# Feed-forward weights decoded without GpSimd, and the norms of blocks 1 and 2 on VectorE

## Chip, cores and metric

One core of a Trainium2 chip. The metric is the device time of one execution of the whole program in microseconds (us), as the median of several runs. TensorE multiplies matrices, VectorE and ScalarE work elementwise, GpSimd too; SyncE only issues DMAs here. A kernel instance has one queue per engine, and each engine takes its instructions in the order of its queue.

## What is computed

Three stages follow each other on 8 batches of 576 tokens and 512 features. First a linear attention: softmax of q over the features and of k over the tokens, in 8 heads of 64. Then a feed-forward stage, which is the one that matters here:

```python
X = np.fft.fft(np.fft.fft(x, axis=1), axis=2)
u = x + np.real(X)
un = (u - mean(u)) / np.sqrt(var(u) + 1e-06)
x = u + np.maximum(un @ w_ch1, 0.0) @ w_ch2     # 512 -> 2048 -> 512
```

Last a gated stage: two token-shift mixes, `k = max(xk @ w_k, 0)`, and the output `sigmoid(xr @ w_r) * (k*k @ w_v)`. The weights arrive as float64 and are read by the kernel as pairs of 32-bit words.

## The kernel before, in words

The 4608 tokens are cut into nine blocks of 512. `front_x` does the attention of batch after batch, `front_y` the two Fourier transforms as matrix products (`transform`) and then the norm of each block whose batches are done (`norm`), `front_z` the feed-forward weights. These are generators. They are stepped by hand before the blocks, until the norm of block 0 and the first six weight pieces are issued (lines 971 to 978), and later by `side()` between the matrix products of the blocks (`mm1`, `mm2`), so that attention and transforms of later batches lie beside the feed-forward products of earlier blocks. This gives the order in which work is traced. A scheduler of the framework then orders the queue of each engine: work traced earlier has priority, work traced later fills in. Batch 1's attention is traced after block 0's norm and the weights, and can be placed among them.

Feed-forward weights: each of the 32 pieces (16 of `w_ch1`, 16 of `w_ch2`, 128 x 512) is loaded as 512 pairs of words into one of four places. `decoded` (line 178) makes a float32 bit pattern of each pair: ScalarE turns the low word into a number of 0 to 7 (L194), VectorE shifts and masks the high word (L195), then merges the sign and top bit (L196), and GpSimd adds the low part (L197). `squares` (L202) then sums each piece's squares on ScalarE; after all 16 pieces of a matrix `scales` makes its power-of-two scale (L211 to L221). `split` (line 223) writes each piece as two float16 parts, high and rest, into a place whose last reader is the split before it:

```python
if c % 4 == 1:
    nc.scalar.activation(out=h, in_=st, func=AF.Copy, scale=s)
    nc.vector.scalar_tensor_tensor(out=l, in0=st, scalar=s, in1=h, op0=ALU.mult, op1=ALU.subtract)
else:
    nc.scalar.activation(out=st, in_=st, func=AF.Copy, scale=s)
    nc.scalar.activation(out=h, in_=st, func=AF.Copy)
    nc.gpsimd.tensor_tensor(out=l, in0=st, in1=h, op=ALU.subtract)
```

These are L229, L230 (8 pieces) and L232, L233, L234 (24 pieces). The first products of a block (L1034) need the normed tokens in two float16 parts (`halves_part`, L642 on ScalarE and L643 on VectorE) and a split `w_ch1`; the second products (L1057) need a split `w_ch2`.

Norms: `norm_part` sums a token's features (L577, L579), takes the mean off (L589), squares on ScalarE (L591, L592), sums again (L595, L596), makes the reciprocal root (L611 to L626) and multiplies (L629). In block 0 TensorE does the sums and VectorE the product. For blocks 1 and 2 sums and product are on GpSimd; from block 3 on the sums are on GpSimd, the product on VectorE. Blocks 0 and 1 go in two parts of 256 tokens, the rest whole.

GpSimd has other work too: a subtraction or product for three halves of the attention (L329, L343), the maximum over partitions for batches 3 to 7 (L323, traced in the front strand), and one step in the decoding of the last stage's weights (`decode`, L167).

Of the kernel before, what the change touches and what calls it, by code (L numbers as in the profile page):

```python
# [13 lines left out]
AF = mybir.ActivationFunctionType  # L14
ALU = mybir.AluOpType
# [15 lines left out]

MAX_PE = (0, 1, 2)

POOL_N = (1, 2)
SUMS_PE = (0,)
SUMS_F32 = (0, 1)

# [7 lines left out]
def net(ctx, tc, q, k, v, w1, w2, mu_k, mu_r, w_k, w_v, w_r, ce_d, se_d, cs_d, ss_d, alt_d, id_d, out):  # L45
    nc = tc.nc
# [18 lines left out]
    def aside(first, strand):  # L65


        turn_of[0] += 1
        if not first:
            return bank(f"side{turn_of[0] % 2 if done_block[0] < 0 else strand}", 1)  # L70
        x = turn_of[0] % 6
        return bank(f"side{x // 3}", 1) if x in (0, 3) else bank(f"acc{(1, 2, 4, 5).index(x)}", 1)
# [3 lines left out]
    def segments(i):  # L76

        t0, n = blocks[i]
        done, found = 0, []
        while done < n:  # L80
            b, s = divmod(t0 + done, S)
            m = min(n - done, S - s)
            found.append((b, s, m, done))
            done += m
        return found
# [86 lines left out]
    def spare_words():  # L172

        if not spare:
            spare.append(up.tile([128, 4, S], F32, tag="u", name="words").rearrange("p t s -> p (t s)").bitcast(U32))
        return spare[0]

    def decoded(w, c):


        z = places[0] % 4
        places[0] += 1
        if z < 2:
            raw = wst.tile([128, 512, 2], U32, tag="raw", name="raw", bufs=2)
        else:
            raw = spare_words()[:, 1024 * (z - 2):1024 * (z - 1)].rearrange("p (n w) -> p n w", w=2)
        if w == 0:
            src = w1.bitcast(U32)[128 * (c % 4):128 * (c % 4) + 128, 1024 * (c // 4):1024 * (c // 4) + 1024]
        else:
            src = w2.bitcast(U32)[128 * c:128 * c + 128, :]  # L190
        nc.sync.dma_start(out=raw.rearrange("p n w -> p (n w)"), in_=src)
        x = wr[:, place[w, c] + 1]
        hi, lo = raw[:, :, 1], raw[:, :, 0]
        nc.scalar.activation(out=lo, in_=lo, func=AF.Copy, scale=2.0 ** -29)  # L194
        nc.vector.tensor_scalar(out=x, in0=hi, scalar1=3, scalar2=0x3FFFFFFF, op0=ALU.logical_shift_left, op1=ALU.bitwise_and)  # L195
        nc.vector.scalar_tensor_tensor(out=x, in0=hi, scalar=0xC0000000, in1=x, op0=ALU.bitwise_and, op1=ALU.bitwise_or)  # L196
        nc.gpsimd.tensor_tensor(out=x, in0=x, in1=lo, op=ALU.add)  # L197

    def squares(w, c):

# [22 lines left out]
    def split(w, c):  # L223
        k = place[w, c]
        st = wr[:, k + 1].bitcast(F32)
        s = wsc[:, 3 * w + 1:3 * w + 2]
        h, l = wf[:, k, 0:512], wf[:, k, 512:1024]
        if c % 4 == 1:
            nc.scalar.activation(out=h, in_=st, func=AF.Copy, scale=s)  # L229
            nc.vector.scalar_tensor_tensor(out=l, in0=st, scalar=s, in1=h, op0=ALU.mult, op1=ALU.subtract)  # L230
        else:
            nc.scalar.activation(out=st, in_=st, func=AF.Copy, scale=s)  # L232
            nc.scalar.activation(out=h, in_=st, func=AF.Copy)  # L233
            nc.gpsimd.tensor_tensor(out=l, in0=st, in1=h, op=ALU.subtract)  # L234

    def w1t(t, f):

# [39 lines left out]
    def mark(name, *ins):  # L277
        marks[name] = ins
# [277 lines left out]
    def mean(i, sq, cs, n):  # L556

        pt = aside(i == 0, 1)
        if i < 2:
            mm(out=pt[:, 0:n], lhsT=ones, rhs=sq[:, 0, cs], start=True, stop=True)  # L560
        else:
            hl = hp.tile([128, 2, 512], F32R, tag="rs", name="hl", bufs=1)
            h, l = hl[:, 0, cs], hl[:, 1, cs]
            nc.scalar.activation(out=h, in_=sq[:, 0, cs], func=AF.Copy)
            nc.vector.tensor_tensor(out=l, in0=sq[:, 0, cs], in1=h.bitcast(F32), op=ALU.subtract)
            mm(out=pt[:, 0:n], lhsT=onesr, rhs=h, start=True, stop=False)
            mm(out=pt[:, 0:n], lhsT=onesr, rhs=l, start=False, stop=True)
        return pt

    def norm_part(i, sq, d, rs, c0, n):  # L570
        segs = [(b, s + max(c0 - o, 0), min(o + m, c0 + n) - max(o, c0), max(o, c0)) for b, s, m, o in segments(i) if o < c0 + n and o + m > c0]
        cs = slice(c0, c0 + n)
        tt = nc.vector.tensor_tensor
        add = nc.gpsimd.tensor_tensor if i else tt
        onpe = i in SUMS_PE
        for b, s, m, o in segs if not onpe else ():
            add(out=sq[:, 0:2, o:o + m], in0=U[b][:, 0:2, s:s + m], in1=U[b][:, 2:4, s:s + m], op=ALU.add)  # L577
        if not onpe:
            add(out=sq[:, 0, cs], in0=sq[:, 0, cs], in1=sq[:, 1, cs], op=ALU.add)  # L579
            yield 0  # L580
            yield 0
            pt = mean(i, sq, cs, n)
        else:
            pt = aside(i == 0, 1)
            for b, s, m, o in segs:
                for t in range(4):
                    mm(out=pt[:, o - c0:o - c0 + m], lhsT=ones, rhs=U[b][:, t, s:s + m], start=(t == 0), stop=(t == 3))
        for b, s, m, o in segs:
            mv = tt(out=d[:, :, o:o + m], in0=U[b][:, :, s:s + m], in1=pt[:, None, o - c0:o - c0 + m].to_broadcast([128, 4, m]), op=ALU.subtract)  # L589
        yield 1  # L590
        nc.scalar.activation(out=sq[:, 0:2, cs], in_=d[:, 0:2, cs], func=AF.Square)  # L591
        ma = nc.scalar.activation(out=sq[:, 2:4, cs], in_=d[:, 2:4, cs], func=AF.Square)  # L592
        yield 0
        if not onpe:
            add(out=sq[:, 0:2, cs], in0=sq[:, 0:2, cs], in1=sq[:, 2:4, cs], op=ALU.add)  # L595
            add(out=sq[:, 0, cs], in0=sq[:, 0, cs], in1=sq[:, 1, cs], op=ALU.add)  # L596
            yield 0
            yield 0
            pt = mean(i, sq, cs, n)
        else:  # L600
            pt = aside(i == 0, 1)
            for t in range(4):
                mp = mm(out=pt[:, 0:n], lhsT=ones, rhs=sq[:, t, cs], start=(t == 0), stop=(t == 3))
            if i == 0:
                mark(5, mv, ma, mp)
        if rs is None:
            rs = hp.tile([128, 2, 512], F32, tag="rs", name="rs", bufs=1)
        v, r = rs[:, 0, cs], rs[:, 1, cs]
        w = sq[:, 1, cs]
        if i in SUMS_F32:  # L610
            nc.scalar.activation(out=r, in_=pt[:, 0:n], func=AF.Ln, bias=wsc[:, 7:8])  # L611
            nc.scalar.activation(out=r, in_=r, func=AF.Exp, scale=-0.5)
            yield 1
            tt(out=v, in0=r, in1=r, op=ALU.mult)
            nc.vector.scalar_tensor_tensor(out=v, in0=pt[:, 0:n], scalar=1e-6, in1=v, op0=ALU.add, op1=ALU.mult)
            nc.vector.tensor_scalar(out=v, in0=v, scalar1=-0.5, scalar2=1.5, op0=ALU.mult, op1=ALU.add)
            tt(out=r, in0=r, in1=v, op=ALU.mult)
        else:
            nc.vector.tensor_scalar(out=v, in0=pt[:, 0:n], scalar1=1e-6, scalar2=None, op0=ALU.add)
            nc.scalar.activation(out=r, in_=v, func=AF.Ln)  # L620
            nc.scalar.activation(out=r, in_=r, func=AF.Exp, scale=-0.5)
            yield 1

            tt(out=w, in0=r, in1=r, op=ALU.mult)
            nc.vector.scalar_tensor_tensor(out=w, in0=w, scalar=-0.5, in1=v, op0=ALU.mult, op1=ALU.mult)
            nc.vector.scalar_tensor_tensor(out=r, in0=w, scalar=1.5, in1=r, op0=ALU.add, op1=ALU.mult)  # L626
        yield 0
        for x in range(2):
            (nc.gpsimd.tensor_tensor if i in POOL_N else tt)(out=d[:, 2 * x:2 * x + 2, cs], in0=d[:, 2 * x:2 * x + 2, cs], in1=r[:, None, :].to_broadcast([128, 2, n]), op=ALU.mult)  # L629
            yield 0  # L630
        if i == 0:
            halves_part(0, c0, n)
# [291 lines left out]
    def front_z():  # L924
        for w in range(2):
            for c in range(17):
                if c < 16:
                    decoded(w, c)
                if c > 0:
                    squares(w, c - 1)  # L930
                yield 0
            scales(w)
            yield 0
        for c in range(4):
            split(0, c)
            yield 0
        for c in range(2):
            split(1, c)
            yield 0
# [387 lines left out]
```

## Time and profile before

| | us |
|---|---|
| median of 3 runs | 1511.14 (1507.36 to 1512.99) |
| the profiled execution, its own time | 1508.74 |
| its span, first to last instruction | 1507.0 |
| TensorE busy in the span | 1413.3 |
| VectorE busy | 1018.2 |
| ScalarE busy | 677.1 |
| GpSimd busy | 224.2 |

The profiled execution took 1.7 us outside its span. An engine counts as busy while an instruction of it runs, and an instruction that is held up after its start counts as running. The granted clock of TensorE is a share of full speed (2.4 GHz), mean 0.971 over the span.

### The profile page before, as it was taken

How to read it: one execution, taken by the hardware profiler on the slowest of the kernel's cores; microseconds unless marked ns; L12 is line 12 of the kernel's file. 1: busy time of each engine (PE TensorE's matmuls, PEld its weight loads, DVE VectorE, ACT ScalarE, POOL GpSimd, SP SyncE). 2: the span in 40 equal slices, each digit the busy share in tenths (PEclk: the TensorE clock that was granted, in tenths of full speed). 3: DMA queues.
4: the chain of work that ended last, by engine and by line, in shares of the span. 5: the costliest groups of instructions: out<-in, count | busy, mean ns of one | idle time of the engine just before them, and what ended most of it. 6: DMA issues, size and time to landing. Idle time of an engine off the chain costs nothing. (4 is left out here: it accounts for less than half of the span.)

```text
span 1507.0 us, 21074 instructions
## 1 busy us (share of the span) xinstructions
PE 1413.3 (94%) x8453; PEld 879.8 (58%) x8453; DVE 1018.2 (68%) x1770; ACT 677.1 (45%) x1237; POOL 224.2 (15%) x180
## 2 busy tenths in 40 slices
PE   3464999999999999999999999999999999999998
PEld 2343888879655655555555444444666666666665
DVE  6997747758477485674452457775899789776643
ACT  5568544434233333332321236554666556564432
POOL 1553532022020010100100204311000000000000
PEclk8586999999999999999999999999999999999999
DMA  8462003211102111101001103410211011100001
GB/s 307 153 219 92 1 1 107 70 50 51 62 16 78 36 48 44 50 34 44 1 11 46 37 29 119 137 46 4 80 35 49 31 57 57 36 22 29 29 15 42
DMA packets 38237, 89.47 MB, mean 59 GB/s; under 512 B 5083, under 2 KB 11516, under 8 KB 38140
## 3 DMA queue, kind: packets, MB, share of 16 engines
q1 hardware_dynamic: 38140, 88.14, 17.2%
q8 instruction: 66, 1.08, 0.3%
q14 instruction: 31, 0.25, 0.1%
HBM read 69.25 MB, written 18.87 MB: 58 GB/s over the span
## 5 line engine op out<-in xcount | busy, mean ns | idle before, releaser
L1034 PE MATMUL h<-unh,wr 128*128 128x512 f16 (+1 forms) x1408 | 381.6, 342 | 1.1 <-ACT unh L642 1.1
L1057 PE MATMUL acc<-hh,wr 128*128 128x512 f16 (+1 forms) x1408 | 370.9, 342 | 3.2 <-DVE wkl L748 2.7
L1034 PEld LDWEIGHTS <-wr 128*128 128x128 f16 x2112 | 203.5, 98 | 171.8 <-issue 11.7
L1057 PEld LDWEIGHTS <-wr 128*128 128x128 f16 x2112 | 203.4, 98 | 164.3 <-DVE wkl L748 3.0
L1034 PE MATMUL h<-unl,wr 128*128 128x512 f16 (+1 forms) x704 | 240.6, 342 | 5.2 <-DVE unl L643 5.2
L1057 PE MATMUL acc<-hl,wr 128*128 128x512 f16 (+1 forms) x704 | 221.5, 342 | 0.0
L1160 PE MATMUL acc<-ring,last 128*128 128x512 f16 x864 | 201.2, 379 | 0.2 <-DVE last L1191 0.2
L1040 DVE SCALAR_TENSOR_TENSOR hl<-h,hh 128x512 f16<-128x512 f32 x144 | 99.1, 688 | 144.5 <-ACT hh L1039 143.5
L1039 ACT ACTIVATE hh<-h 128x512 f16<-128x512 f32 x144 | 85.2, 592 | 162.7 <-PE h L1034 162.4
L1160 PEld LDWEIGHTS <-last 128*128 128x128 f16 x864 | 84.0, 98 | 86.5 <-DVE last L1191 0.7
L1095 PEld LDWEIGHTS <-wkh 128*128 128x128 f16 x1008 | 98.5, 98 | 34.1
L1148 PE MATMUL side<-ring,x 128*128 128x512 f16 x432 | 101.1, 379 | 0.0
L1189 ACT ACTIVATE last<-last,pw 128x512 f32<-128x512 f32 x72 | 51.6, 717 | 106.9 <-DVE last L1188 106.3
L1095 PE MATMUL h<-x,wkh 128*128 128x256 f16 x560 | 95.7, 273 | 0.0
L1110 DVE TENSOR_TENSOR last<-h,last 128x512 f32<-128x512 f32 x90 | 61.8, 687 | 49.9 <-PE h L1095 49.8
L1095 PE MATMUL h<-x,wkl 128*128 128x256 f16 x280 | 76.3, 273 | 0.0
L1095 PE MATMUL h<-last,wkh 128*128 128x256 f16 x448 | 76.1, 273 | 0.0
L1148 PEld LDWEIGHTS <-x 128*128 128x128 f16 x432 | 42.3, 98 | 42.5
L1191 DVE TENSOR_TENSOR last<-last 128x512 f16<-128x512 f32 x72 | 49.4, 687 | 22.1 <-ACT last L1190 21.7
L1095 PE MATMUL h<-last,wkl 128*128 128x256 f16 x224 | 61.1, 273 | 0.0
L577 POOL TENSOR_TENSOR sq<-u 128x384 f32<-128x384 f32 (+7 forms) x16 | 24.9, 1558 | 209.5 <-DVE u L522 100.8
L854 ACT ACTIVATE aa<-y,ms 128x512 f32<-128x512 f32 x72 | 48.0, 712 | 17.5 <-DVE x L862 12.2
(349 smaller groups left out, 2298.9 us busy)
## 6 DMA issues: line engine op xcount, KB each, us to landing
vt<-in_v_dram SPq DMA_DIRECT2D x16, 650.0 KB, 5.0
kt<-in_k_dram SPq DMA_DIRECT2D x16, 576.0 KB, 3.9
qt<-in_q_dram SPq DMA_DIRECT2D x16, 576.0 KB, 3.9
out_dram<-oo SPq DMA_DIRECT2D x36, 256.0 KB, 2.0
y<-yT SPq DMA_DIRECT2D x8, 1026.0 KB, 5.3
raw<-in_w_dram SPq DMA_DIRECT2D x16, 512.0 KB, 3.8
words<-in_w_dram SPq DMA_DIRECT2D x16, 512.0 KB, 4.5
raw<-in_w_k_dram SPq DMA_DIRECT2D x16, 256.0 KB, 3.5
```

The lines of the kernel that those rows point to most:

```text
L577: add(out=sq[:, 0:2, o:o + m], in0=U[b][:, 0:2, s:s + m], in1=U[b][:, 2:4, s:s + m], op=ALU.add)
L854: nc.scalar.activation(out=a, in_=y[:, t, 0:n], func=AF.Copy, scale=mu[:, w, 1, t:t + 1])
L1034: mm(out=pt[:, o:o + m], lhsT=a, rhs=c[:, t, o:o + m], start=(t == z == 0), stop=(t == 3 and z == 2))
L1039: ma = nc.scalar.activation(out=hh[:, 0:n], in_=pt[:, 0:n], func=AF.Relu)
L1040: mv = nc.vector.scalar_tensor_tensor(out=hl[:, 0:n], in0=pt[:, 0:n], scalar=0.0, in1=hh[:, 0:n], op0=ALU.max, op1=ALU.subtract)
L1057: mm(out=acc[x][:, o:o + m], lhsT=a, rhs=c[:, o:o + m], start=(f == z == o == 0), stop=(f == NF - 1 and z == 2), skip_group_check=(i < 2))
L1095: mm(out=pt[:, 256 * x:256 * x + 256], lhsT=c[:, u, 128 * x:128 * x + 128], rhs=d[:, u], start=(fresh and x == u == z == 0), stop=(last an ...
L1110: nc.vector.tensor_tensor(out=out, in0=view(pt), in1=addend, op=ALU.add)
L1148: mm(out=pt, lhsT=a[:, v, u, c, o:o + 128], rhs=w[:, t, :], start=(t == y == 0), stop=(t == 3 and y == 2))
L1160: mm(out=acc[x], lhsT=a[:, 128 * x:128 * x + 128], rhs=c[:, f, :], start=(f == z == 0), stop=(f == 7 and z == 2))
L1189: nc.scalar.activation(out=o, in_=o, func=AF.Square, scale=W["pw"][:, 10 + g:11 + g])
L1191: nc.vector.tensor_tensor(out=l2, in0=o, in1=h2, op=ALU.subtract)
```

## The change

The set of blocks whose product is on GpSimd becomes empty, and the sums go to GpSimd only from block 3 on. In `decoded` ScalarE's scale and bias are chosen so that the low part comes out complemented to 7, and VectorE puts it into the three free low bits with an exclusive-or and an or in one instruction; the instruction on GpSimd goes. In `split` all 32 pieces take the form that eight had. `decode`, for the last stage's weights, stays as it is.

```diff
-POOL_N = (1, 2)
+POOL_N = ()
...
-        nc.scalar.activation(out=lo, in_=lo, func=AF.Copy, scale=2.0 ** -29)
+        nc.scalar.activation(out=lo, in_=lo, func=AF.Copy, scale=-0.9975 * 2.0 ** -29, bias=7.49)
...
-        nc.gpsimd.tensor_tensor(out=x, in0=x, in1=lo, op=ALU.add)
+        nc.vector.scalar_tensor_tensor(out=x, in0=lo, scalar=7, in1=x, op0=ALU.bitwise_xor, op1=ALU.bitwise_or)
...
-        if c % 4 == 1:
-            nc.scalar.activation(out=h, in_=st, func=AF.Copy, scale=s)
-            nc.vector.scalar_tensor_tensor(out=l, in0=st, scalar=s, in1=h, op0=ALU.mult, op1=ALU.subtract)
-        else:
-            nc.scalar.activation(out=st, in_=st, func=AF.Copy, scale=s)
-            nc.scalar.activation(out=h, in_=st, func=AF.Copy)
-            nc.gpsimd.tensor_tensor(out=l, in0=st, in1=h, op=ALU.subtract)
+        nc.scalar.activation(out=h, in_=st, func=AF.Copy, scale=s)
+        nc.vector.scalar_tensor_tensor(out=l, in0=st, scalar=s, in1=h, op0=ALU.mult, op1=ALU.subtract)
...
-        add = nc.gpsimd.tensor_tensor if i else tt
+        add = nc.gpsimd.tensor_tensor if i > 2 else tt
```

## Rows read from the trace of the kernel before

**Rows 1.** The page, part 1: busy us (share of the span) xinstructions.
```profile
PE 1413.3 (94%) x8453; PEld 879.8 (58%) x8453; DVE 1018.2 (68%) x1770; ACT 677.1 (45%) x1237; POOL 224.2 (15%) x180
```

**Rows 2.** Busy time by stretch: length, PE, PEld, DVE, ACT, POOL, PEclk, DMA share, GB/s.
```profile
28.00:136.00 108.00, 50.57 (x203) 38.08 (x201) 103.55 (x156) 73.17 (x160) 56.68 (x36) 0.65 0.50 166
136.00:210.00 74.00, 69.22 (x563) 60.43 (x563) 40.12 (x73) 43.89 (x82) 33.34 (x25) 0.96 0.08 26
210.00:260.00 50.00, 50.00 (x436) 44.52 (x434) 33.60 (x59) 20.11 (x33) 13.96 (x13) 1.00 0.20 65
```

**Rows 3.** Timeline, 118 to 140 us: start, us, engine, line; [idle before <-releaser].
```profile
133.74 0.37 PE L1034 MATMUL h<-unl,wr 128*128 128x256 f16 x1 [5.23 <-DVE unl L643]
```

**Rows 4.** The same view, GpSimd and VectorE, 118 to 140 us.
```profile
128.90 1.34 POOL L197 TENSOR_TENSOR wr<-wr,words 128x512 uint32<-128x512 uint32 x1 [1.28 <-ACT unh L642]
129.02 1.77 DVE L196 SCALAR_TENSOR_TENSOR wr<-words,wr 128x512 uint32<-128x512 uint32 x1
```

**Rows 5.** VectorE's groups by form, 28 to 136 us: xcount | busy us, mean ns.
```profile
L196 DVE SCALAR_TENSOR_TENSOR wr<-raw,wr 128x512 uint32<-128x512 uint32 x16 | 14.3, 893 | 0.1
L196 DVE SCALAR_TENSOR_TENSOR wr<-words,wr 128x512 uint32<-128x512 uint32 x16 | 13.7, 874 | 0.0
L195 DVE TENSOR_SCALAR wr<-words 128x512 uint32<-128x512 uint32 x16 | 11.0, 692 | 2.0 <-DMA words<-in_w_dram 1.9
L195 DVE TENSOR_SCALAR wr<-raw 128x512 uint32<-128x512 uint32 x16 | 10.6, 662 | 0.8 <-DMA raw<-in_w_dram 0.8
L435 DVE TENSOR_TENSOR eo<-u 128x288 f32<-128x288 f32 x8 | 5.2, 695 | 0.0
L629 DVE TENSOR_TENSOR d<-d,rs 128x512 f32<-128x512 f32 x4 | 4.7, 1226 | 0.0
...
L307 DVE TENSOR_REDUCE m<-kt 128x256 f32<-128x1024 f32 x2 | 3.9, 1970 | 0.1
...
L451 DVE TENSOR_TENSOR el<-eo,eh 128x289 fp32r<-128x289 f32 x4 | 2.9, 723 | 0.0
...
L319 DVE TENSOR_TENSOR m<-ident,wsc 128x256 f32<-128x256 f32 x2 | 1.9, 966 | 0.0
L617 DVE TENSOR_TENSOR rs<-rs 128x256 f32<-128x256 f32 x2 | 1.9, 962 | 0.0
L614 DVE TENSOR_TENSOR rs<-rs 128x256 f32<-128x256 f32 x2 | 1.9, 956 | 0.0
...
L359 DVE COPY kvbd<-kvbd 64x2 f32<-64x2 f32 x1 | 1.2, 1236 | 0.0
...
L513 DVE TENSOR_TENSOR sd<-pc,acc 128x290 f32<-128x290 f32 x2 | 0.9, 452 | 0.0
...
L490 DVE TENSOR_TENSOR yl<-acc,yh 128x256 fp32r<-128x256 f32 x2 | 0.8, 419 | 0.0
```

**Rows 6.** Lines L195, L196 and L230 alone: duration ns min/median/max.
```profile
L195 DVE TENSOR_SCALAR wr<-raw x16: 399/415/1516, 27.9 to 121.0; 128x512 uint32<-128x512 uint32 x16
L196 DVE SCALAR_TENSOR_TENSOR wr<-raw,wr x16: 675/680/1708, 28.3 to 125.2; 128x512 uint32<-128x512 uint32 x16
L230 DVE SCALAR_TENSOR_TENSOR wr<-wr,wsc x8: 739/752/2285, 134.2 to 200.6; 128x512 f16<-128x512 f32 x8
```

**Rows 7.** Timeline, VectorE, a pair of merges back to back.
```profile
42.40 1.29 DVE L196 SCALAR_TENSOR_TENSOR wr<-words,wr 128x512 uint32<-128x512 uint32 x2
```

**Rows 8.** Timeline, 312 to 348 us, VectorE, GpSimd and TensorE.
```profile
332.60 1.23 DVE L333 TENSOR_TENSOR kt<-kt,m 128x1024 f32<-128x1024 f32 x1 [3.39 <-POOL m L323]
...
324.23 1.34 POOL L596 TENSOR_TENSOR sq<-sq 128x512 f32<-128x512 f32 x1
331.48 1.08 POOL L323 PARTITION_ALL_REDUCE m<-m  x1 [5.92 <-issue]
...
335.52 0.33 PE L386 MATMUL side<-ident,qt 128*128 128x128 f32 x1 [2.69 <-DVE qTl L377]
```

**Rows 9.** TensorE's groups by line, 128 to 350 us, last column the idle time before them.
```profile
L320 PE MATMUL side<-m,one 128*128 128x256 f32 x6 | 1.9, 397 | 1.6 <-DVE m L319 1.6
```

## The prediction

> **What bounds the kernel now.** The page's busy times come first [rows 1]: TensorE is busy 1413.3 of 1507.0 us, so the program is bound by TensorE wherever that engine is dense, and the whole program can only lose the 94 us in which TensorE stands still, plus what the slow clock costs. Busy time by stretch shows where those are [rows 2]. From 28 to 136 us TensorE is busy 50.6 of 108 us at a granted clock of 0.65, that is, at times on the lower of its two levels, 1.2 GHz; from 136 on it is busy 69.2 of 74 and then 50.0 of 50, at 0.96 and 1.00. In the front stretch VectorE is the full engine, 103.6 of 108. The timeline says what opens the dense stage: the first products with the low half of the normed tokens start at 133.7, after 5.2 us of waiting for VectorE [rows 3]. So the time is the moment at which VectorE has worked through the front, plus TensorE work that this change doesn't touch, plus the few gaps left behind 136 us.
>
> **How much of VectorE's front is work.** While GpSimd's L197 ran from 128.90 to 130.24, an L196 that started at 129.02 took 1.77 us [rows 4], against a median of 0.68 [rows 6]; it ended 0.55 after GpSimd did. So an instruction of VectorE that reads two tensors of SBUF stands still while GpSimd adds two tensors, and counts as busy. L195 has one input and a median of 0.415, and at worst took 1.52 [rows 6]. A product that reads PSUM (L513, 0.45) shows no such excess [rows 5]. I therefore take mean minus undisturbed time, times the count, for each group [rows 5, 6]:
> L195: 11.0 + 10.6 - 32 x 0.415 = 8.3. L196: 14.3 + 13.7 - 32 x 0.68 = 6.2. L435, 8 x (0.695 - 0.452, L513 of the same width) = 1.9. L629, 4 x (1.226 - 0.68, 512 wide as L196) = 2.2. L451, 4 x (0.723 - 0.452) = 1.1. L319, L617 and L614, two each, against L490 of their width (0.419): 1.1 each, 3.3. L359, at least 1.236 - 0.452 = 0.8. Together 23.8 us of standing still.
>
> **Decoding (32 pieces, all in the front).** GpSimd loses L197, and with it the 23.8 us, since the groups held up lie where L197 is nearly all that GpSimd does. VectorE gains 32 instructions of the shape and kind of L196. Two of those back to back took 1.29 [rows 7], so the second one costs a step of 0.61: 32 x 0.61 = 19.5 us. Combining two bit operations, as L196 does, I take the same price; above it I bound it by the full 0.68 (21.8 in all), and below by L195's 0.415 (13.3), which reads one tensor; it reads two, so L196's is the near one. ScalarE's L194 gets a bias, for which I count nothing: ScalarE is idle 35 of the 108 us [rows 2]. Without that cover even a tenth of a us on each would be 3 us. No DMA is added or moved on SyncE's queue.
>
> **Splits (24 of 32 change form).** ScalarE loses one of two instructions per piece, GpSimd its subtraction, VectorE gains an L230, median 0.75 [rows 6]; its step on the queue I take as 0.07 less, as in the pair of L196, 0.68. Two of the 24 fall in the front: +1.4. The other 22 cost 15 us on VectorE between 136 and 210, where it is idle 34 us and TensorE has work [rows 2]; I count them at nothing. If that cover failed, up to 15 us would show. ScalarE now waits for VectorE instead of GpSimd before the high half of the next piece, because that half overwrites what the subtraction reads; behind it in ScalarE's queue are the copies out of PSUM that TensorE waits for. For this stage GpSimd's subtractions also held VectorE: the slowest L230 took 2.29 against 0.75 [rows 6], and TensorE stood 1.6 us for an L319 in this strand [rows 9]. I take back 0.9 of those 1.6, that is all but one added split of 0.68; the ends are 1.6 and nothing.
>
> **Norms of blocks 1 and 2.** Each has some 5,100 elements per partition to add and multiply. By L490 (256 in 0.42) and L196 (512 in 0.68) these come to some 7 us per block on VectorE. A part of 128 columns of it (L577) comes before 136 us: I take 0.3. The rest lies where VectorE is idle 16 of 50 us [rows 2]; I count it at nothing, and 7 us per block if the cover is gone. In block 2 something is freed: GpSimd's reduction over partitions L323 started 5.9 us after the L596 before it ended, with nothing that the profile shows to wait for, and VectorE stood 3.4 us for it, then TensorE 2.7 us for a copy (L377) queued behind [rows 8]. With L595 and L596 off GpSimd the reduction follows another reduction, and can start when its input is there. I take the 2.7 us as gained; the ends are 2.7 and nothing, if L377 is then late for VectorE's own sums.
>
> **Sum.** Front: 19.5 + 1.4 + 0.3 - 23.8 = -2.6. Behind it: -2.7 - 0.9. Together -6.2 us. Against the profiled execution, 1508.7 us (span 1507.0, 1.7 around it), that is 1502.5; the median of the runs is 2.4 us higher, so 1511.1 - 6.2 = 1504.9 us. A measurement can tell some 0.5%, 7.6 us, from no change, so the forecast lies just within that.
>
> **A rule that speaks against it.** The Trainium skill (Perfetto Trace Analysis, section Identifying the Most-Contended Engine) judges VectorE by occupancy and says that the fullest engine is the one to relieve. By that rule the front's VectorE, 96% occupied, should be given nothing, and adding 21 us to it would end the front 21 us later. The row on L196 under GpSimd speaks against it, as occupancy here holds time in which the engine stood.
>
> **Rivals.**
> *A, the order changes (more gained).* Batch 1's attention, traced after the weights, has both its L307 in the front [rows 5]. With more work of higher priority on VectorE, some of it may be pushed behind the start of the dense stage, where VectorE has room. For it: it is ready early only to fill in. Against it: it was placed in the front although VectorE is 96% full. If as much is pushed out as comes in, the front ends earlier by all 23.8, less the TensorE work that then has to be done later at full clock. I take 14 to 24 us gained: 1487 to 1497.
>
> *B, no net change.* VectorE's stills may be replaced by waits for ScalarE or TensorE along the chain transform, norm, halves, since in one strict queue each link waits for the one before. For it: TensorE idles in the front for many short waits, not one. Against: VectorE was idle only 4.4 us in 108, so hardly any link waits for something else. Change of -3 to +4: 1508 to 1515.
>
> *C, slower.* The added 21.2 us on VectorE's queue lie ahead of norm 0's links and the stills were mostly spent in instructions off that path. For it: 14.5 of the 23.8 us are in the decoding's own L195 and L196, not in the norm. Against: the queue is in order, so a stall of any instruction delays all behind it. With the gains behind the front kept (3.6), the kernel gets slower by over 7.6 us once less than 10.0 of the 23.8 us are saved (21.2 - 3.6 - 10.0 = 7.6); with none saved it is +17.6: 1519 to 1529.
>
> *D, it does less than it says.* The low part could come out late: the merge needs ScalarE's L194 as GpSimd did, and if VectorE waits there, all waits. This is part of B.
>
> **Chances.** Forecast 0.50, its own range 1499 to 1508, of which about half is beyond the 0.5% bound; A 0.20; B 0.17; C 0.13. Faster by over 0.5%: 0.24 + 0.20 = 0.44. Within 0.5%: 0.26 + 0.17 = 0.43. Slower: 0.13. The range takes in A but for its last step and all of B, and leaves out C and a little at the low end: 1488 to 1515.
>
> **What would show it.** Right: in the front no L195 or L196 above some 0.8 us, the new merge near 0.68, VectorE's busy time between 28 us and the dense start lower by a few us, the first low-half product a few us before 133.7, and no 2.7 us gap before an L386 at the end of norm 2. Rival A: batch 1's second L307 behind the first L1034. Rival B: idle time on VectorE in the front well above 4 us. Rival C: the first low-half product after 140. Wrong in its size: a merge above 0.9 us, or new gaps of TensorE before L1057 for a split. A TensorE gap in blocks 1 and 2 for L629 or L642 would show that the norms' cover was not there.

## Result, and the profile after

The changed kernel takes 1521.9 us (median of 4 runs, 1520.5 to 1522.5), against 1510.3 for the kernel before on the same chip: ratio 1.0076, interval 1.0063 to 1.009. It is slower by 11.6 us where 6.2 us less was forecast. The profiled execution took 1521.51 us, 1519.7 of them span. (Two experiments, e1 and e4, had some executions of 2.6 to 5.1 ms, far outside all others; their ratios and times leave those out.)

The page's busy times, beside [rows 1]:

```profile
PE 1415.3 (93%) x8453; PEld 879.5 (58%) x8453; DVE 1032.9 (68%) x1846; ACT 667.1 (44%) x1213; POOL 115.3 (8%) x104
```

GpSimd loses 109 us, VectorE gains 15, and TensorE's 8453 instructions take 2.0 us more. Where TensorE stands still I get by summing the gaps between its instructions in the two traces, split at the first product with the low half of the normed tokens: 69.9 us up to there and 12.5 behind it before, 65.0 and 28.5 after. So the front gained 4.9 us, and 16.0 us were lost behind it; with the 2.0 that is the longer span (12.7) to within 0.4, most of it at the two ends.

**The front gained, by more than was forecast.** The first product with the low half starts at 128.19 us, 5.5 us before 133.74 [rows 3]; 2.6 were forecast. VectorE's groups by form, 28 to 136 us, after (compare [rows 5]; L430 and L624 were L435 and L629):

```profile
L197 DVE SCALAR_TENSOR_TENSOR wr<-raw,wr 128x512 uint32<-128x512 uint32 x16 | 10.9, 684 | 0.1
L196 DVE SCALAR_TENSOR_TENSOR wr<-raw,wr 128x512 uint32<-128x512 uint32 x16 | 10.9, 683 | 0.0
...
L430 DVE TENSOR_TENSOR eo<-u 128x288 f32<-128x288 f32 x8 | 3.2, 452 | 0.0
...
L624 DVE TENSOR_TENSOR d<-d,rs 128x512 f32<-128x512 f32 x4 | 2.6, 688 | 0.0
```

Each of these is back at the undisturbed time that the prediction took for it: L196 from 893 ns to 683, L624 from 1226 to 688, L430 from 695 to 452. The new L197 takes 684 ns; the timeline has 0.60 us from the end of the instruction before it to its own end, so 32 of them lengthen the queue by 19.3 us.

Busy time by stretch, after (columns as in [rows 2]):

```profile
28.00:136.00 108.00, 55.59 (x253) 43.74 (x252) 101.77 (x203) 69.42 (x154) 2.17 (x1) 0.67 0.49 166
136.00:210.00 74.00, 72.11 (x611) 62.48 (x610) 51.07 (x89) 37.62 (x69) 4.62 (x2) 1.00 0.08 26
210.00:260.00 50.00, 44.50 (x365) 38.73 (x364) 37.71 (x71) 18.80 (x32) 0.00 (x0) 0.97 0.25 87
...
132.00:136.00 4.00, 4.00 (x40) 3.74 (x38) 2.68 (x9) 2.38 (x4) 0.00 (x0) 1.00 0.00 0
...
517.00:528.00 11.00, 0.36 (x2) 0.28 (x1) 2.04 (x4) 0.99 (x2) 2.33 (x2) 0.64 0.00 0
528.00:540.00 12.00, 12.00 (x45) 5.27 (x45) 6.75 (x9) 5.15 (x8) 3.62 (x2) 0.76 0.16 51
```

The same view of the kernel before, at the places to compare:

```profile
136.00:140.00 4.00, 3.75 (x19) 3.53 (x19) 1.07 (x8) 2.33 (x4) 1.57 (x2) 0.50 0.00 0
140.00:144.00 4.00, 4.00 (x32) 3.75 (x32) 0.91 (x4) 4.00 (x8) 0.76 (x1) 0.82 0.29 52
...
517.00:528.00 11.00, 11.00 (x59) 5.91 (x57) 6.97 (x11) 4.97 (x8) 2.53 (x2) 1.00 0.10 21
528.00:540.00 12.00, 12.00 (x59) 5.97 (x58) 8.94 (x10) 5.48 (x8) 3.62 (x2) 1.00 0.08 31
```

In the front the granted clock reaches its upper level some 10 us earlier: it is 1.00 from 132 on (2.4 GHz), where before it was still 0.50 until 140 (1.2 GHz). But from 210 to 260 TensorE now stands 5.5 us (before: none), and from 517 to 528 it stands almost all of 11 us where it was full. In the 12 us behind that gap the clock is 0.76, so 12 x 0.24 = 2.9 us of full-speed work is lost on top of the gap.

The gaps, on the timeline of TensorE, after ([idle before <-releaser]):

```profile
128.19 0.37 PE L1029 MATMUL h<-unl,wr 128*128 128x256 f16 x1 [2.16 <-DVE unl L638]
...
249.94 0.67 PE L555 MATMUL side<-sq,onesr 128*128 128x256 f32 x2 [4.69 <-DVE kt L331]
...
527.69 0.79 PE L561 MATMUL side<-hl,onesr 128*128 128x512 f32 x1 [10.64 <-ACT hl L559]
...
636.79 0.80 PE L561 MATMUL side<-hl,onesr 128*128 128x512 f32 x1 [4.55 <-ACT hl L559]
```

The first is the dense start, 133.74 before [rows 3]. The three others make 19.9 us; no gap behind the dense start was above 2.8 us before. (That one, 2.75 us in the last stage, is 3.60 now.) Two wait for the first sum of a later block, that of its features (blocks 4 and 5, still on GpSimd in both kernels), one for the PSUM tile `side`.

**Why block 4's sum is late.** GpSimd's timeline from 495 us, before and then after (L323 is L318 after, L577 is L572, L579 is L574):

```profile
514.73 1.06 POOL L323 PARTITION_ALL_REDUCE m<-m  x1 [54.25 <-DVE m L310]
522.79 1.27 POOL L577 TENSOR_TENSOR sq<-u 128x512 f32<-128x512 f32 x1 [7.00 <-DVE u L523]
524.14 1.26 POOL L579 TENSOR_TENSOR sq<-sq 128x512 f32<-128x512 f32 x1
```

```profile
509.90 1.71 POOL L572 TENSOR_TENSOR sq<-u 128x512 f32<-128x512 f32 x1 [51.58 <-DVE u L517]
517.36 1.08 POOL L318 PARTITION_ALL_REDUCE m<-m  x1 [5.75 <-issue]
525.73 1.25 POOL L574 TENSOR_TENSOR sq<-sq 128x512 f32<-128x512 f32 x1 [7.28 <-issue]
...
625.21 1.54 POOL L318 PARTITION_ALL_REDUCE m<-m  x1 [55.88 <-DVE m L305]
633.75 0.98 POOL L572 TENSOR_TENSOR sq<-u 128x384 f32<-128x384 f32 x1 [7.01 <-issue]
```

None of these lines of code was changed; their order was. The scheduler now puts the attention's reduction over partitions between the two additions of block 4's sum. GpSimd then stands 5.75 us before the reduction and 7.28 us before the next addition, with nothing that the profile shows to wait for. The first addition ends at 511.6, the second starts at 525.7; with them next to each other, as before, this is 0.1 us.

Block 5 is another case: there the reduction stands in front of the sum in both kernels. Before, it started at 618.79 us, and the input of the addition behind it (L523 on VectorE) ended at 626.63, only 0.8 us ahead of the addition:

```profile
627.44 0.99 POOL L577 TENSOR_TENSOR sq<-u 128x384 f32<-128x384 f32 x1 [7.58 <-DVE u L523]
```

After, the reduction starts at 625.21, and the addition's input (L518 on VectorE) ends at 626.91. So L572 starts 7.01 us after the reduction's end and 6.8 us after its input: the same step on GpSimd, but no longer beside a wait for the input.

**Why L555 is late.** VectorE's timeline, after:

```profile
244.25 0.74 DVE L1070 SCALAR_TENSOR_TENSOR u<-acc,wsc,u 128x512 f32<-128x512 f32 x1
244.91 1.28 DVE L624 TENSOR_TENSOR d<-d,rs 128x512 f32<-128x512 f32 x2
246.11 2.06 DVE L1070 SCALAR_TENSOR_TENSOR u<-acc,wsc,u 128x512 f32<-128x512 f32 x3
248.09 1.21 DVE L328 TENSOR_TENSOR kt<-kt,side 128x1024 f32<-128x1024 f32 x1
249.21 0.57 DVE L331 TENSOR_TENSOR kt<-kt,side 64x128 f32<-64x128 f32 x2
```

L328 and L331 read `side`, and TensorE's L555 overwrites it. They stand behind block 0's residual additions (L1070) and a product of norm 1 (L624, 1.2 us, new on VectorE). Before, the same two (L333, L336) ran 14 us ahead of the first L1075:

```profile
246.84 1.21 DVE L333 TENSOR_TENSOR kt<-kt,side 128x1024 f32<-128x1024 f32 x1
...
260.79 0.75 DVE L1075 SCALAR_TENSOR_TENSOR u<-acc,wsc,u 128x512 f32<-128x512 f32 x1
```

### The profile page after: what moved, and what is told of

Read it like the earlier page. It is cut to its first block, busy times and chain, and to the rows that moved or that the text cites. A ratio compares the mean times of both kernels' runs of the same rounds, so it can differ in the third digit from the quotient of the medians.

```text
span 1519.7 us, 21029 instructions
## 1 busy us (share of the span) xinstructions
PE 1415.3 (93%) x8453; PEld 879.5 (58%) x8453; DVE 1032.9 (68%) x1846; ACT 667.1 (44%) x1213; POOL 115.3 (8%) x104
## 3 DMA queue, kind: packets, MB, share of 16 engines
q8 instruction: 66, 1.08, 0.3%
## 5 line engine op out<-in xcount | busy, mean ns | idle before, releaser
L849 ACT ACTIVATE aa<-y,ms 128x512 f32<-128x512 f32 x72 | 48.0, 711 | 17.4 <-DVE x L857 12.2
L853 DVE SCALAR_TENSOR_TENSOR aa<-y,ms,aa 128x512 f32<-128x512 f32 x72 | 54.0, 769 | 1.2
```

The source lines that it names most:

```text
L849: nc.scalar.activation(out=a, in_=y[:, t, 0:n], func=AF.Copy, scale=mu[:, w, 1, t:t + 1])
L853: nc.vector.scalar_tensor_tensor(out=a, in0=y[:, t, 1:n + 1], scalar=mu[:, w, 0, t:t + 1], in1=a, op0=ALU.mult, op1=ALU.add)
```

## Experiments

All ratios are against the kernel before on the same chip (medians 1510.6 for e1 to e4, 1511.3 for e5 to e8, 1510.8 for e9 to e11; 1510.3 beside the changed kernel). Where a run is set against the changed kernel, the two medians are compared, and they come from comparisons on different chips, so such a difference can be off by about 1 us.

**e1_decode**: the kernel before with the decoding alone.

```diff
-        nc.scalar.activation(out=lo, in_=lo, func=AF.Copy, scale=2.0 ** -29)
+        nc.scalar.activation(out=lo, in_=lo, func=AF.Copy, scale=-0.9975 * 2.0 ** -29, bias=7.49)
-        nc.gpsimd.tensor_tensor(out=x, in0=x, in1=lo, op=ALU.add)
+        nc.vector.scalar_tensor_tensor(out=x, in0=lo, scalar=7, in1=x, op0=ALU.bitwise_xor, op1=ALU.bitwise_or)
```

> The kernel before with only the decoding moved to VectorE. Theory (the front gains, and the loss of the whole change is a GpSimd queue order in blocks 4 and 5): the dense stage starts some 4 to 6 us earlier than in the kernel before, no gap of TensorE over 4 us behind it, time 0.997 (0.994 to 1.000) of before. Rival (VectorE's added 20 us of work is what costs): dense stage later, 1.004 or more.

Measured: 1501.2 us (three executions), ratio 0.9943 [0.9924, 0.9961], that is 8.6 us less. The first low-half product comes 4.6 us earlier; the term for the decoding was 23.8 - 19.5 = 4.3. Another part is the clock. TensorE's timeline and the busy time by stretch, e1:

```profile
129.10 0.37 PE L1034 MATMUL h<-unl,wr 128*128 128x256 f16 x1 [0.91 <-DVE unl L643]
```

```profile
128.00:132.00 4.00, 3.09 (x16) 2.18 (x15) 3.33 (x8) 3.02 (x9) 0.91 (x1) 0.50 0.00 0
132.00:136.00 4.00, 3.76 (x29) 3.36 (x26) 1.30 (x8) 3.60 (x7) 1.37 (x2) 0.86 0.00 0
136.00:140.00 4.00, 3.84 (x32) 3.20 (x32) 0.13 (x1) 4.00 (x8) 0.10 (x1) 1.00 0.92 314
```

A clock that changes from 0.50 to 1.00 once and has a mean of 0.86 from 132 to 136 changes at 133.1; before, with 0.82 from 140 to 144, at 141.4. At half speed the stretch from the dense start to there costs (133.1 - 129.1) / 2 = 2.0 us here and (141.4 - 133.7) / 2 = 3.8 before, so 1.8 us are gained beside the 4.6. TensorE's busy time falls by 4.4 us in all, to 1408.9, with the same instructions; the other 2.6 of it I can't assign to a place. (Between executions of the kernel before alone the mean granted clock varies from 0.965 to 0.974, so a part may be no effect of the edit.)

**e2_split**: the splits alone (24 pieces in the form of the other 8).

```diff
-        if c % 4 == 1:
...
-        else:
-            nc.scalar.activation(out=st, in_=st, func=AF.Copy, scale=s)
-            nc.scalar.activation(out=h, in_=st, func=AF.Copy)
-            nc.gpsimd.tensor_tensor(out=l, in0=st, in1=h, op=ALU.subtract)
```

> The kernel before with only the split of 24 pieces moved from GpSimd to VectorE. Theory: 0.998 to 1.002, no gap over 4 us of TensorE in blocks 4 and 5, because the queue of GpSimd there has the reduction over partitions ahead of both sums of a block. Rival (ScalarE and VectorE wait for each other in block 0): new gaps of TensorE before 260 us, 1.003 or more.

Measured: 1516.0 us, 1.0029 [1.0016, 1.0043], that is 4.4 us more: the expectation missed, and the rival's gap came. The dense start is 2.6 us later, and a gap before L555 is there. Behind the dense start TensorE stands 4.8 us more than before (17.4 against 12.5): the 3.21 below and 2.42 in front of an attention product at 276.9 are the new ones. Timeline of TensorE and VectorE, e2:

```profile
256.39 1.21 DVE L328 TENSOR_TENSOR kt<-kt,side 128x1024 f32<-128x1024 f32 x1
...
258.24 1.19 PE L555 MATMUL side<-sq,onesr 128*128 128x256 f32 x2 [3.21 <-DVE kt L331]
```

L328 stands right behind all four residual additions (L1070) here too, but without norm 1's product, which is on GpSimd in e2; the gap is 1.5 us shorter than the changed kernel's 4.69.

**e3_norm**: the norms alone.

```diff
-POOL_N = (1, 2)
+POOL_N = ()
-        add = nc.gpsimd.tensor_tensor if i else tt
+        add = nc.gpsimd.tensor_tensor if i > 2 else tt
```

> The kernel before with only the norms of blocks 1 and 2 moved to VectorE. Theory: the gap of some 5 us before the mean of block 1 or 2 (245 us in the changed kernel), since the product on VectorE comes ahead of the reader of a PSUM bank, shows here too: +2 to +5 us; less the 2.7 us gap at the end of norm 2; no gap over 4 us in blocks 4 and 5: 0.998 to 1.003. Rival (the norms alone carry the loss): 1.006 or more.

Measured: 1504.5 us, 0.9963 [0.9952, 0.9974], that is 5.6 us less. The 2.69 us gap of [rows 8] is gone, and no gap before L555 (here L560) is there: that part of the expectation was wrong.

So the three parts by themselves make -8.6, +4.4 and -5.6, in all -9.8 us; together they make +11.6. Some 21 us are of their company.

**e4_pair_kept**: the changed kernel, with one order of GpSimd's queue put back: the reductions over partitions that come after block 4's sum in the program wait behind it.

```diff
+    summed = [None]
...
+                with tc.issue_after(summed[0].ins) if summed[0] else ExitStack():
-                nc.gpsimd.partition_all_reduce(out_ap=m, in_ap=m, channels=128, reduce_op=bass_isa.ReduceOp.max)
+                    nc.gpsimd.partition_all_reduce(out_ap=m, in_ap=m, channels=128, reduce_op=bass_isa.ReduceOp.max)
...
-            add(out=sq[:, 0, cs], in0=sq[:, 0, cs], in1=sq[:, 1, cs], op=ALU.add)
+            summed_now = add(out=sq[:, 0, cs], in0=sq[:, 0, cs], in1=sq[:, 1, cs], op=ALU.add)
+            if i == 4:
+                summed[0] = summed_now
```

> The changed kernel, but in block 4 the reduction over partitions is queued behind the second addition of the first sum, so that the two additions stand together. Theory: the 10.6 us gap of TensorE at 517 us falls to under 3 us, and the time by 7 to 10 us against the changed kernel: 1.000 to 1.003 of before. Rival (TensorE would wait there anyway, for VectorE or the mean): gap over 7 us, 1.006 or more.

Measured: 1507.6 us, 0.998 [0.9969, 0.9991]: 14.3 us less than the changed kernel, from an order alone, and more than the 7 to 10 expected. **e9_pair_kept_look** is the same kernel again, for its profile.

> The kernel of e4 once more, for a profile at the usual clock. Theory: no gap of TensorE over 3 us before block 4's first mean, the two additions there back to back; time 1504 to 1509 as in e4's runs.

Measured: 1506.9 us. GpSimd's timeline, e9 (lines shifted by 3):

```profile
512.10 1.71 POOL L575 TENSOR_TENSOR sq<-u 128x512 f32<-128x512 f32 x1 [58.49 <-DVE u L520]
513.89 1.26 POOL L577 TENSOR_TENSOR sq<-sq 128x512 f32<-128x512 f32 x1
521.04 1.08 POOL L321 PARTITION_ALL_REDUCE m<-m  x1 [5.89 <-issue]
```

The two additions are 0.1 us apart and the 10.64 us gap is gone. So is the one of 4.55: the queue behind block 4 shifted too, and the 14.3 us belong to both gaps, less the new ones. The gap before L555 (here L558) stays, 4.65 us, and new ones come in: 1.19 us for ScalarE's work on k behind the later reduction, and 1.85 us for a copy of VectorE.

**e5_all_sums**: the changed kernel with the sums of all blocks on VectorE, so that no addition stands beside a reduction.

```diff
-        add = nc.gpsimd.tensor_tensor if i > 2 else tt
+        add = tt
```

> The changed kernel with the sums of all nine blocks on VectorE, so that GpSimd has only reductions over partitions from 262 us until the last weights and never changes its library between them. Theory: both gaps of TensorE before a mean (10.6 us at 517, 4.6 us at 632) are gone and no L323-like wait replaces them, the 4.7 us gap at 245 us stays; 10 to 16 us under the changed kernel, 0.997 to 1.001 of before. Rival (VectorE is what runs late, so 40 us more on it makes it worse): 1.008 or more.

Measured: 1499.6 us, 0.9926 [0.9912, 0.9941], 22.3 us less than the changed kernel where 10 to 16 were expected. (GpSimd does not keep to reductions alone here: between 355 and 649 us a MEMSET of the Fourier strand, L457, 0.33 us, still stands between them four times, and the reduction behind it starts 7.0 to 8.9 us later; TensorE has no gap over 0.4 us there.) No gap at 517 or 632; TensorE's timeline still has the third:

```profile
250.91 1.19 PE L555 MATMUL side<-sq,onesr 128*128 128x256 f32 x2 [4.61 <-DVE kt L331]
```

**e6_decode_norm**: decoding and norms (the diffs of e1 and e3), splits as before.

> The kernel before with decoding and norms moved, the splits as before. Theory (the parts add up where the queue of GpSimd keeps its order, as it does here): 0.9943 and 0.9963 give 0.990 to 0.993 of before, some 1496 us; the reduction stands ahead of both sums of block 4. Rival (any two parts together collide): over 0.996.

Measured: 1498.4 us, 0.9917 [0.99, 0.9934]. TensorE stands only 9.9 us behind the dense start; before block 4's first mean it stands 0.90, and its longest gap is 2.97, in the last stage. GpSimd's timeline:

```profile
505.63 1.06 POOL L323 PARTITION_ALL_REDUCE m<-m  x1 [55.07 <-DVE m L310]
514.18 1.25 POOL L577 TENSOR_TENSOR sq<-u 128x512 f32<-128x512 f32 x1 [7.48 <-issue]
```

The order is that of the kernel before: one step of 7.48 us in front of the pair, where it is all but covered (0.90 us). Against e6, the changed kernel adds the splits alone, and they cost 1521.9 - 1498.4 = 23.5 us.

**e7_split_norm**: splits and norms (the diffs of e2 and e3), decoding as before.

> The kernel before with splits and norms moved, the decoding as before. GpSimd's queue has the reduction between the two additions of block 4's first sum here, as in the changed kernel. Theory: a gap of TensorE of 8 to 12 us before that block's first mean, and a time 8 to 12 us over the 1510 that the two parts give when added (1515.98 + 1504.54 - 1510.57), so some 1518 to 1522. Rival (the gap needs all three parts): no gap over 5 us there, about 1510.

Measured (one execution): 1524.7 us, 2.7 above the expected range. The order is the changed kernel's; timeline of GpSimd and TensorE, e7:

```profile
515.84 1.72 POOL L572 TENSOR_TENSOR sq<-u 128x512 f32<-128x512 f32 x1 [51.52 <-DVE u L517]
523.25 1.08 POOL L318 PARTITION_ALL_REDUCE m<-m  x1 [5.70 <-issue]
531.06 1.25 POOL L574 TENSOR_TENSOR sq<-sq 128x512 f32<-128x512 f32 x1 [6.73 <-issue]
533.02 0.80 PE L561 MATMUL side<-hl,onesr 128*128 128x512 f32 x1 [9.82 <-ACT hl L559]
```

So the order comes with splits and norms together, and doesn't need the decoding. Alone, neither brings it: in e2 and in e3 the reduction stands ahead of both additions. Splits with decoding, without the norms, were not run.

**e8_extra_reduction**: the kernel before, with one more reduction over partitions (one column of `amax`, 0.38 us long; its result is read by nothing) between the two additions of block 4.

```diff
+            half_sum = add(...)
...
+            es = ExitStack()
+            if i == 4:
+                with tc.issue_after(half_sum.ins):
+                    extra = nc.gpsimd.partition_all_reduce(out_ap=amax[:, 0, 0:1], in_ap=amax[:, 0, 0:1], channels=128, reduce_op=bass_isa.ReduceOp.max)
+                es.enter_context(tc.issue_after(extra.ins))
+            with es:
+                add(...)
```

> The kernel before with one more reduction over partitions, of one column that nothing reads afterwards, queued on GpSimd between the two additions of block 4's first sum. Theory: the addition after it starts some 13 us later than the one before it ended (5.8 us to the reduction, about 7 behind it), TensorE stands 9 to 13 us before that block's first mean, the kernel is 9 to 13 us slower. Rival (only the reduction's own time counts): 1 to 2 us slower.

Measured (one execution): 1523.3 us, 12.0 more than the kernel before. Timeline, e8:

```profile
523.41 1.27 POOL L577 TENSOR_TENSOR sq<-u 128x512 f32<-128x512 f32 x1 [6.70 <-DVE u L522]
530.47 0.38 POOL L582 PARTITION_ALL_REDUCE amax<-amax  x1 [5.79 <-issue]
538.05 1.25 POOL L585 TENSOR_TENSOR sq<-sq 128x512 f32<-128x512 f32 x1 [7.20 <-issue]
540.01 0.80 PE L566 MATMUL side<-hl,onesr 128*128 128x512 f32 x1 [10.37 <-ACT hl L564]
```

A reduction of 0.38 us in this place of the queue, with nothing else changed, makes the gap of TensorE: 5.79 us to go into it and 7.20 to come back.

**e10_subtract_only**: the kernel before, the 24 subtractions on VectorE, ScalarE keeping both its instructions.

```diff
-            nc.gpsimd.tensor_tensor(out=l, in0=st, in1=h, op=ALU.subtract)
+            nc.vector.tensor_tensor(out=l, in0=st, in1=h, op=ALU.subtract)
```

> The kernel before with only the 24 subtractions of the splits moved from GpSimd to VectorE, while ScalarE keeps both of its instructions per piece. Theory (what the new split costs, 5 us alone, comes from ScalarE's relief: pieces are ready earlier, block 0's residual additions move ahead of a reader of a PSUM bank in VectorE's queue): no gap of TensorE over 2 us near 255 us, 0.997 to 1.001 of before. Rival (VectorE's 24 more instructions cost it): gap of 3 us or more there, 1.002 or more.

Measured: 1514.3 us, 1.0026 [1.0016, 1.0037], that is 3.9 us more than the kernel before. The gap before L555 is not there, so that one comes only where ScalarE has one instruction less (e2, e5, e7, e9 and the changed kernel have it; e1, e3, e6, e8, e10 and e11 don't). But the cost of the splits by themselves stays, in the rival's size and without its gap: the expectation was half wrong. In this kernel the dense start is 1.6 us later and a strand of the attention is late; timeline of TensorE, e10:

```profile
273.59 1.16 PE L348 MATMUL side<-vt,kt 128*128 128x130 f32 x8 [3.40 <-ACT kt L337]
```

The subtraction that L337 reads (L333 on VectorE) starts at 270.63 us here and started at 265.31 before; the wait for L337 was 0.54 us. VectorE's busy time from 136 to 210 us rose from 40.1 to 51.6 us here and to 54.3 in e2. That the strand is late because of this is likely, but no run isolates it.

**e11_decode_norm_all_sums**: e6 with the sums of all blocks on VectorE (`add = tt`).

> The kernel of e6 (decoding and norms moved, splits as before) with the sums of all blocks on VectorE, so that GpSimd's library is not changed between 262 us and the last weights. Theory: e6 lost only 0.9 us before a mean in block 4, so little is left to gain: 0.988 to 0.992 of before. Rival (VectorE too full in the blocks): over 0.994.

Measured: 1494.9 us, 0.9905 [0.9882, 0.9928]: the best of all, 15.9 us under the kernel before and 27 under the changed one, as expected. GpSimd has the MEMSETs between its reductions here too, as in e5. TensorE stands 8.0 us behind the dense start.

## Why the prediction was wrong

**Decoding: right, in its mechanism too.** Every group that was counted as held up came down to the time that the prediction took for it, and the merge, priced at a step of 0.61 us, took 0.60 on the queue. In e1 VectorE's busy time from 28 us to the dense start fell from 101.3 to 97.3 us with some 20 us of work added, so some 24 us of standing went, against 23.8 counted. The term -4.3 is e1's -4.6 at the dense start. Missing was what an earlier start does to the clock: in e1 it reaches its upper level 8 us earlier, worth 1.8 us by the working above. [Rows 2] had 0.96 there and the prediction gave it no term.

**The other two terms of the front** were off: the splits (+1.4) moved the dense start by 2.6 us alone (e2), the norms (+0.3) by -0.9 (e3, 132.84). With the three together it came 5.5 us earlier, not 2.6; the rest of that difference is not shown.

**The rule on occupancy: it misleads here.** The Trainium skill, Perfetto Trace Analysis, section Identifying the Most-Contended Engine, takes occupancy of VectorE as a fair measure of how near it is to its limit. Read so, as the prediction did, 21 us more on a VectorE 96% occupied would end the front 21 us later. It ended 5.5 us earlier (128.19 against 133.74), because by the count above 23.8 of the 103.6 occupied us were standing.

**Rivals.** A: batch 1's second L302 is at 115.34, ahead of the dense stage, so nothing was pushed out of the front. B wanted idle time on VectorE well above 4 us in the front; from 28 us to the dense start it was 105.7 - 101.3 = 4.4 before and is 100.2 - 95.4 = 4.8. C wanted the first low-half product after 140, and it came at 128.19: the time, 1521.9, lies within C's 1519 to 1529, but not by its mechanism, and so by luck.

**Gaps behind 136 us.** The 2.69 us before L386 are gone, as forecast, and the 0.9 for L320 are not; TensorE's groups by line, 128 to 350 us, after:

```profile
L555 PE MATMUL side<-sq,onesr 128*128 128x256 f32 x8 | 2.5, 390 | 4.7 <-DVE kt L331 4.7
...
L315 PE MATMUL side<-m,one 128*128 128x256 f32 x6 | 1.9, 397 | 1.5 <-DVE m L314 1.5
...
L381 PE MATMUL side<-ident,qt 128*128 128x128 f32 x5 | 1.4, 284 | 0.2 <-ACT qT L370 0.2
```

L315 stands 1.5 us as L320 did [rows 9]. The norms, counted at -2.4 in all, brought -5.6 alone (e3): their own work was covered there, as the prediction said, with no gap for the product or the halves. In the changed kernel TensorE waits for neither by name, but 1.2 us of norm 1's product stand ahead of L328 in the 4.69 us before L555.

**The step that failed** is that of the splits: "The other 22 cost 15 us on VectorE between 136 and 210, where it is idle 34 us and TensorE has work [rows 2]; I count them at nothing." The cover was counted as a sum of idle time, and the price as at most 15 us in that stretch. Alone the splits cost 4.4 us (e2). On top of decoding and norms they cost 23.5 (changed kernel against e6), and on top of the norms alone 20.2 (e7, one execution, against e3). Most of it falls 300 us and more behind the splits, in queues whose code they don't touch. Since the norms gain alone and lose 8.7 us on top of the splits (e7 against e2), the loss belongs to the two together; the sum that took each part by itself had no place for it. Changed kernel against e6 comes out: TensorE stands 18.6 us more behind the dense start than in e6 (28.5 against 9.9) and 0.6 less ahead of it, and is busy 4.8 us more (1415.3 against 1410.5) with the same instructions, 2.9 of it by the clock of 0.76 from 528 to 540 us, where e6 has 1.00; that makes 22.8 of the 23.0 us between the spans.

Behind this lies an assumption that the prediction made only in one direction: an order that changes was rival A, a gain. That a program is listed by a scheduler, and that an edit that shifts due times shifts the order of all queues behind it, had no rival on the slow side. It could have been priced from [rows 8]: the reduction L323 starts 5.92 us after the addition ahead of it with nothing to wait for. The prediction read that as a stall that goes if the additions go, and did not ask what it costs if another pair of the two kinds meets. By e4 and e8 it is the larger part: one reduction put between two additions costs 12.0 us (e8), taken out of there gains 14.3 (e4, with the gap in block 5).

Open is which due time of the scheduler turns the order, why ScalarE's relief puts L328 behind L1070, and what the splits' own 4 us consist of: the later dense start and the late attention strand are seen, but no run isolates their cause.

## What to carry to other kernels

Where a scheduler lists the program, an edit is not done when its own terms are summed: compare the order of every engine's queue before and after, also far from the edit, and price each new neighbour. On GpSimd, keep reductions over partitions and elementwise operations from alternating where another engine waits for them (e4, e8), or take the elementwise work that is waited for off it (e5, e11). Test the parts of a change alone and in pairs: two of the three parts here were gains, and the third costs five times as much in company as alone.

## What the runs showed of the hardware

GpSimd stands between an elementwise operation and a reduction over partitions, without an instruction and with its inputs ready; the profile shows idle time with "issue" as its end. Over all such places in the runs, 200 to 700 us, the way into the reduction took 5.70 to 6.01 us ten times (5.70 in e7, 5.75 after, 5.92 in [rows 8]) and 7.83 to 8.53 us three times, the way back 6.73 to 7.54 us in fifteen. In e8, with a reduction of 0.38 us in place of one of 1.08, the two steps were as long: 5.79 and 7.20. The Trainium skill, GPSIMD Engine Reference, section Instruction dispatch, gives some 6 us, measured as 5.95, for the first call to a freshly loaded kernel with no visible instruction. Most ways in agree with it in size; that code is loaded there, no run here shows, and the way back is longer than that figure.

A gap of TensorE costs more than its length: behind the 10.64 us the granted clock was 0.76 for the next 12 us, behind e8's 10.37 us it was 0.74 from 540 to 552 us.
